# A three-instruction split of a row maximum, and the place of a tanh, in an attention kernel with a gated bilinear branch

## The chip, the cores and the metric

The kernel runs on one core of a Trainium2 chip. The metric is the device time of one execution in microseconds (us), the median of several runs. A core has five engines that run at the same time, each with its own instruction queue in order: TensorE (PE in the profile, with PEld for its weight loads), VectorE (DVE), ScalarE (ACT), GpSimd (POOL) and SyncE (SP), which here issues the DMAs.

## The reference

```python
xn = layernorm(x)                                # x: 2048 tokens x 512, fp32
qkv = xn @ wqkv                                  # 32 heads of 16
p = softmax(q @ k.T * 16 ** -0.5)                # for each head, 2048 x 2048
s = (p @ v) @ wo
h = (xn @ w_gate) * (xn @ w_up)                  # 2048 x 1792
g = silu(h @ w_down)
return x + s * g
```

All inputs and the output are fp32. `silu(y)` is computed as `y * (0.5 * tanh(y / 2) + 0.5)`.

## The kernel before, in words

**Splitting.** fp32 operands of matmuls are cut into a rounded high part (type fp32r) and a rest, and a product is made of high by high, high by low and low by high. For scores the three products stand under each other in 48 rows of one matmul (`KB = 48`). Two more rows of the contraction (`KR = 50`) take the row maximum off: the key side holds ones there, the query side the negated maximum, again as a rounded part and a rest.

**Units.** Heads are taken in 8 groups of four, queries in 4 chunks of 512: 32 units `i`. Each unit has 64 *positions*: 16 key tiles (`kt`) of 128 by four heads (`j`). `position` (function below) issues for each one a matmul `t` (keys by queries with the maximum, 50 rows, line L631) and its exponential on ScalarE into a tile `e` (L633), and, 86 positions ahead of it (`LEAD`), a matmul `s` for the scores of a later unit (48 rows, L609), whose maximum over 512 keys VectorE takes straight from PSUM into `MX` (L611). The matmuls `t` write to three rotating PSUM banks (`st`), the matmuls `s` to three others.

**Maxima.** When the last score of a unit has been reduced, `maxima(i)` reduces the four partial maxima of each row to the rounded and to the exact negated maximum (L617, L615), subtracts the two (L618, VectorE, both inputs in SBUF), turns the result by 32x32 blocks (L620), writes it to DRAM (`MD`) and reads it back as rows 48 and 49 of the query tile `qs`. The unit's first `t` stands 22 positions further on.

**Cycles.** The main loop runs 256 cycles. One cycle issues 7, 8 or 9 positions and spreads a share of *filler* matmuls between them (the projections of later heads, then the gated branch, then the output projection); the first and the last position of a cycle have no filler behind them. Then `values` runs what is due on other engines and `block`, the 16 matmuls `pv` (L644) of two key tiles with V. Their result goes to one of the three `st` banks as well and ScalarE copies it out: into the tile `part` (L655), which GpSimd adds to the sum `acc`, or, once for each unit, straight into `acc` (L650). A `pv` block needs the exponentials of its eight positions only, and the cycle's last position always lies behind these.

**The gated branch.** It runs over four chunks of tokens. The last step of a chunk adds two pairs of y tiles (L427), and then puts a generator `silu` on the list `later`: for each of the four token tiles a tanh on ScalarE (L362, from `y` into the tile `e2`, one buffer), two instructions on GpSimd (scale and shift, product with y) and, but for the last chunk, a store to DRAM (`YD`). `step_small(later)` takes one step of it; `position` calls it at `j == 3` and `kt % 4 == 2`, that is every 16 positions, ahead of that position's exponential, wherever in a cycle the position lies. The 16 tanhs lie between 634.39 and 1646.99 us of the span.

**Order.** PE, ACT, DVE and POOL run in the order in which the program is written. The queue of SP is ordered by the framework's scheduler. All SP and POOL instructions are issued from one helper line (L63).

**Constants.** `ones` (128x32) is set by GpSimd at the start; two rows of 2048 ones each are sent from it by DMA into rows 48 and 49 of the key tiles.

Of the kernel before, what the change touches and what calls it, by code (L numbers as in the profile page):

```python
# [11 lines left out]
F32 = mybir.dt.float32  # L12
# [36 lines left out]
def body(ctx, tc, x, wqkv, wo, wg, wu, wd, out):  # L49
# [45 lines left out]
    ones = keep.tile([P, 32], F32, name="ones")  # L95
    eps = keep.tile([P, 1], F32, name="eps")
    pool.memset(eps, 1e-5)
    pool.memset(ones, 1.0)
    V = keep.tile([P, NT, VCOLS], F32, name="V")

    def ones_columns(tts):
# [39 lines left out]
    def run_all(queue):  # L141
        while queue:
            queue.pop(0)()
# [467 lines left out]
        nc.vector.tensor_reduce(MX[i][:, j, t, kc:kc + 1], o, axis=AX.X, op=OP.max)  # L611

    def maxima(i):
        m = keep.tile([P, 4, 4], F32, name="m", bufs=2)
        nc.vector.tensor_reduce(m, MX[i], axis=AX.X, op=OP.max, negate=True)  # L615
        mm = keep.tile([P, 4, 2, 4], F32R, name="mm", bufs=2)
        nc.vector.tensor_reduce(mm[:, :, 0], MX[i], axis=AX.X, op=OP.max, negate=True)  # L617
        nc.vector.tensor_tensor(mm[:, :, 1], m, mm[:, :, 0], op=OP.subtract)  # L618
        mt = keep.tile([P, 32], F32, name="mt", bufs=2)
        nc.vector.transpose(mt, mm.rearrange("p j s t -> p (j s t)").bitcast(F32))  # L620
        dma(MD[i].rearrange("f (b q) -> b f q", b=4), mt)
        md = MD[i].rearrange("(p e s t) q -> e s p (t q)", p=2, e=2, s=2)
        for e in range(2):
            row = 64 * e + KB
            dma(QS[i][row:row + 2].bitcast(F32), md[e])
# [79 lines left out]

    def early():

        nc.scalar.activation(look, ones[0:1, 0:1], AF.Sqrt)
        for tt in range(4):
            load_x(tt)  # L710
        wraw = []
        for which in (1, 0):
            wraw.append(wtile(f"w{which}r"))
            dma(wraw[-1], wqkv[:, which * D:which * D + P].rearrange("(d p) f -> p d f", p=P))
        norm["raws"] = raws = [etile() if d < 3 else part_tile() for d in range(ND)]
        for d in range(ND):
            dma(raws[d], wqkv[d * P:(d + 1) * P, 2 * D:])
        for tt in range(4, NT):
            load_x(tt)

        def ahead(m):
            fst["qk", m] = qk_weights(m, 1), qk_weights(m, 0)

        def exp_table(_):
            nc.scalar.activation(look, ones[0:1, 0:1], AF.Exp)

        def warm(n):
            for _ in range(n):
                nc.tensor.matmul(psum("x", "warm"), ident, idle, start=True, stop=True)

        warm(4)
        first = (0, 1), (2, 3)
        for tts in first:
            ln_open(tts)
        ln_stats(0)
        ln_stats(1)
        ln_root(first[0])
        ln_scale(first[0])
        ln_apply(0)
        ln_apply(1)  # L740
        ln_stats(2)
        ln_stats(3)
        ln_turn(0)
        ln_turn(1)
        warm(3)
        ln_root(first[1])
        ln_scale(first[1])
        ln_apply(2)
        last = ln_apply(3)
        ln_low(0)  # L750
        ln_low(1)
        ln_turn(3)
        ln_turn(2)
        ln_low(3)
        ln_low(2)
        wk, wq = [split_raw(f"w{which}", raw, last) for which, raw in zip((1, 0), wraw)]
        wv = [[etile().bitcast(F32R) for _ in range(ND)] for _ in range(2)]
        for d in range(ND):
            nc.scalar.activation(wv[0][d], raws[d], AF.Copy)
            pool.tensor_tensor(wv[1][d], raws[d], wv[0][d], op=OP.subtract)  # L760

        def k(c):
            yield from qk_proj(wk, 0, 1, c, "f")
            load_k(0, [c])

        def q(c):
            yield from qk_proj(wq, 0, 0, c, "f" if c else "x")
            load_q(c)

        def v(*tts):  # L770
            for tt in tts:
                yield from v_proj(wv, tt, "f")

        at = {n: [] for n in range(253)}
        for c, stats, apply, turns in ((1, (0, 2, 4, 6), (26, 26, 26, 26), (38, 42, 46, 50)),
                                       (2, (16, 20, 26, 27), (60, 60, 62, 62), (70, 74, 79, 83)),
                                       (3, (30, 34, 36, 38), (73, 73, 85, 85), (100, 106, 112, 118))):
            for t in range(4):
                for n, fn in ((stats[t], ln_stats), (apply[t], ln_apply), (turns[t], ln_turn)):
                    at[n].append((fn, 4 * c + t))  # L780
        for tts, n, root, scale in ((tuple(range(4, 8)), 0, 13, 25), (tuple(range(8, NT)), 16, 52, 53)):
            at[n].insert(0, (ln_open, tts))
            at[root].append((ln_root, tts))
            at[scale].insert(0, (ln_scale, tts))
        at[190].append((ones_rows, ks[0]))
        at[150].append((exp_table, None))
        at[205].append((ahead, 1))
        at[130] += [(ones_columns, slice(8, NT)), (other_keys, None)]
        fst["v"] = v_proj(wv, NT - 1, "st")
        gens = [k(0), q(0), v(0, 1, 2), k(1), q(1), v(3), k(2), v(4, 5), k(3), v(*range(6, NT - 1))]  # L790
        scored = 0
        stream = (n for g in gens for n in g)
        for n in range(253):
            for fn, arg in at[n]:
                fn(arg)
            if n in EARLY:
                for _ in range(4 if n != EARLY[-1] else LEAD - scored):
                    score(scored, 0)
                    scored += 1
                if scored == 64:  # L800
                    maxima(0)
            next(stream, None)
        assert scored == LEAD
        return wq
# [29 lines left out]
    def step_small(q):  # L834
        if q and next(q[0], 1):
            q.pop(0)
# [70 lines left out]
            heads.append(finish(rounds[0][0]))  # L907
            step_small(heads)

    ready, reduced = {}, []  # L910

    def position(q):

        n, j = divmod(q, 4)
        i, kt = divmod(n, NT)
        g, c = divmod(i, NC)
        now[0] = n
        Tied.on = n < 18
        if j == 0:
            if kt == 8 and i + 2 < NU:  # L920
                load_q(i + 2)
            if kt == 0 and g + 1 < NG and c == 1:
                load_k(g + 1)
            ready[n] = i, kt, []
        if j == 3 and kt % 4 == 2:
            step_small(later)
        ready[n][2].append(expo(i, kt, j))
        scored = q + LEAD
        if scored < TOTAL:
            score(scored, 1)  # L930
        step()
        if j == 1:
            prepare()
        if scored < TOTAL and scored % (4 * NT) == 4 * NT - 1:
            reduced.append(lambda: maxima(scored // (4 * NT)))
# [3 lines left out]
    with tc.manual_schedule(engines=ORDERED):  # L939
        with banks_of(EARLY_BUFS):  # L940
            fil = Filler(filler(early()), spread)
        ctx.enter_context(banks_of(BUFS))
        run(fst["v"])
        q = 0
        while q < 4:
            position(q)
            q += 1
        for b in range(NU * NT // 2):
            if fil.done:
                parts = iter([3, 2, 3, 2, 2, 2, 1, 2])  # L950
                fil = Filler(ending(), lambda n: next(parts))
            work = fil.begin()
            if b >= NU * NT // 2 - 2:
                last = TOTAL - 4 * (NU * NT // 2 - 1 - b)
            else:
                fits = min(9, max(7, int(2.6 + 0.62 * work))) if q + LEAD < TOTAL and work else 8
                need = 8 * (b + 1)
                last = min(max(q + fits, need + AHEAD[0]), need + AHEAD[-1], TOTAL - 4)
            count = last - q
            fil.spread(max(2, count - 2))  # L960
            for k in range(count):
                position(q)
                q += 1
                if 0 < k < count - 1 or count < 3:
                    fil.part()
            if b < NU * NT // 2 - 1:
                values([ready.pop(2 * b), ready.pop(2 * b + 1)])
        run_all(before_values)
        while heads:
            step_small(heads)  # L970
        block([ready.pop(NU * NT - 2), ready.pop(NU * NT - 1)])
        run_all(behind_values)
        flush()
        while fil.left or not fil.done:
            now[0] += 1
            prepare()
            if not fil.left:
                fil.fetch()
            for _ in range(fil.left):
                next(fil.gen)  # L980
            fil.left = 0
            fil.fetch()
            flush()
# [17 lines left out]
```

## Time and profile before

| what | value |
|---|---|
| median of 3 runs | 1718.5 us (1717.84 to 1718.88) |
| the profiled execution's own time | 1718.17 us |
| its span | 1716.4 us (1.8 us lie around it) |
| granted clock of TensorE | 0.999 of full speed |
| busy: PE, DVE, ACT, POOL | 99%, 84%, 76%, 52% of the span |

A row of the page or of a group view names the line, the engine, the operation, what it writes and reads, the shape and the count; behind the bar stand the busy time in us, the mean of one in ns, and the idle time of the engine just before these instructions with what ended it. A row of the timeline begins with start and duration in us; idle time ahead of the instruction and its releaser stand in brackets. Since PE's matmuls are pipelined and their ends are modelled, PE reads as busy nearly everywhere, and time that it loses has to be read from the distance between its blocks: the copy of a `pv` block (L655 or L650) starts as the block ends, once a cycle, so the distance of two such copies is the length of a cycle.

### The profile page before, as it was taken

The page shows a single profiled execution, that of the slowest core. Times are in us where ns is not written, and L with a number is a line of the kernel's source. Part 1 is how long each engine was busy: PE and PEld are TensorE (multiplying, and loading weights), DVE is VectorE, ACT ScalarE, POOL GpSimd, SP SyncE. Part 2 cuts the span into 40 slices and gives each one's busy share as a digit, 9 for nine tenths or more (in the row PEclk, how much of TensorE's full clock was granted, in tenths as well). Part 3 has the DMA queues.
Part 4 walks back from the last instruction along what each step waited for, and adds up shares of the span by engine and source line. Part 5 has one row for each costly group of instructions (what it writes and reads, how often), then busy time and mean ns, then how long its engine had stood idle before and what let it go on. Part 6 is the DMA issues. An engine that isn't in the chain of part 4 may idle for free. (4 is left out here: it accounts for less than half of the span.)

```text
span 1716.4 us, 35005 instructions
## 1 busy us (share of the span) xinstructions
PE 1705.0 (99%) x13574; PEld 1042.5 (61%) x13574; DVE 1435.9 (84%) x2478; ACT 1307.4 (76%) x2568; POOL 885.4 (52%) x889
## 2 busy tenths in 40 slices
PE   8999999999999999999999999999999999999998
PEld 6666656666666665666656565666665666666655
DVE  6778888888888888888888888888888888898933
ACT  6358877877777778778777777887778787777774
POOL 5315445762644638446354572663637546446572
PEclk9999999999999999999999999999999999999999
DMA  6316633620241312412115220320225112011352
GB/s 210 106 48 201 243 115 125 152 66 19 64 91 36 107 47 73 89 47 60 30 52 133 64 74 23 92 71 27 64 75 125 54 36 73 27 54 48 121 177 79
DMA packets 117378, 145.79 MB, mean 85 GB/s; under 512 B 12636, under 2 KB 74332, under 8 KB 114524
## 3 DMA queue, kind: packets, MB, share of 16 engines
q1 hardware_dynamic: 117212, 143.55, 28.5%
q8 instruction: 107, 1.75, 0.4%
q14 instruction: 59, 0.48, 0.1%
HBM read 95.94 MB, written 47.45 MB: 84 GB/s over the span
## 5 line engine op out<-in xcount | busy, mean ns | idle before, releaser
L611 DVE TENSOR_REDUCE mx<-s 128x1 f32<-128x512 f32 x2048 | 1256.1, 683 | 212.3 <-PE s L609 177.4
L633 ACT ACTIVATE e<-t 128x512 f32<-128x512 f32 x2048 | 1100.1, 601 | 99.2 <-PE pv L644 47.4
L631 PE MATMUL t<-qs,ks 50*128 50x512 f32 x2048 | 783.4, 408 | 0.1
L609 PE MATMUL s<-ks,qs 48*128 48x512 f32 x2048 | 771.0, 410 | 0.6 <-DVE mx L611 0.5
L63 POOL TENSOR_TENSOR acc<-acc,part 128x512 f32<-128x512 f32 x214 | 276.3, 1291 | 610.2 <-ACT part L655 609.8
L631 PEld LDWEIGHTS t<-qs,ks 50*128 50x128 f32 x2048 | 359.1, 185 | 276.0 <-issue 118.6
L644 PE MATMUL pv<-e,V 128*32 128x512 f32 x4096 | 492.5, 598 | 0.0
L609 PEld LDWEIGHTS s<-ks,qs 48*128 48x128 f32 x2048 | 350.6, 185 | 28.8 <-issue 5.4
L655 ACT ACTIVATE part<-pv 128x512 f32<-128x512 f32 x214 | 128.1, 599 | 209.7 <-PE pv L644 209.7
L644 PEld LDWEIGHTS pv<-e,V 128*32 128x32 f32 x4096 | 107.0, 109 | 242.0 <-issue 215.9
L289 PE MATMUL g<-fh,w1h 64*128 64x512 f32 x224 | 90.5, 404 | 0.0
L285 PE MATMUL u<-fh,w0h 64*128 64x512 f32 x224 | 90.4, 404 | 0.0
L289 PE MATMUL y<-dh,hh 64*128 64x512 f32 x224 | 89.6, 400 | 0.0
L285 PE MATMUL y<-dh,hh 64*128 64x512 f32 x224 | 88.9, 397 | 0.0
L289 PE MATMUL u<-fh,w0l 64*128 64x512 f32 x224 | 88.2, 394 | 0.0
L289 PE MATMUL g<-fl,w1h 64*128 64x512 f32 x224 | 88.0, 393 | 0.0
L285 PE MATMUL g<-fl,w1h 64*128 64x512 f32 x224 | 88.0, 393 | 0.0
L285 PE MATMUL u<-fh,w0l 64*128 64x512 f32 x224 | 88.0, 393 | 0.0
L285 PE MATMUL u<-fl,w0h 64*128 64x512 f32 x224 | 88.0, 393 | 0.0
L289 PE MATMUL g<-fh,w1l 64*128 64x512 f32 x224 | 87.9, 393 | 0.0
L285 PE MATMUL g<-fh,w1h 64*128 64x512 f32 x224 | 87.9, 392 | 0.0
L289 PE MATMUL u<-fl,w0h 64*128 64x512 f32 x224 | 87.8, 392 | 0.0
(262 smaller groups left out, 2987.5 us busy)
## 6 DMA issues: line engine op xcount, KB each, us to landing
w1r<-in_wg_dram SPq DMA_DIRECT2D x56, 256.0 KB
w0r<-in_wu_dram SPq DMA_DIRECT2D x56, 256.0 KB
wdr<-in_wd_dram SPq DMA_DIRECT2D x56, 256.0 KB
qs<-QD SPq DMA_DIRECT2D x64, 192.0 KB
ks<-KD SPq DMA_DIRECT2D x12, 768.0 KB
KD<-hl SPq DMA_DIRECT2D x16, 512.0 KB
QD<-hl SPq DMA_DIRECT2D x16, 512.0 KB
OD<-acc SPq DMA_DIRECT2D x31, 256.0 KB
```

The source lines that it names most:

```text
L63: got = getattr(self.engine, name)(*args, **kw)
L285: nc.tensor.matmul(outs[k], l[LOWER], r[LOWER], start=k == 0 and n == 0, stop=(stop or k == 0) and n == len(low) - 1, skip_group_check=k == 1)
L289: nc.tensor.matmul(outs[1 - k], l[UPPER], r[UPPER], start=k == 0 and m == 0, stop=(stop or k == 0) and m == len(high) - 1, skip_group_chec ...
L609: nc.tensor.matmul(o, QS[i][b:b + KB, pr, t * P:(t + 1) * P], k[b:b + KB, pr, kc * 512:(kc + 1) * 512], start=True, stop=True)
L611: nc.vector.tensor_reduce(MX[i][:, j, t, kc:kc + 1], o, axis=AX.X, op=OP.max)
L631: nc.tensor.matmul(o, k[b:b + KR, pr, kt * P:(kt + 1) * P], QS[i][b:b + KR, pr], start=True, stop=True)
L633: nc.scalar.activation(e, o, AF.Exp, scale=DH ** -0.5)
L644: nc.tensor.matmul(o[32 * j:32 * j + 32], V[:, kt, h0:h0 + 32], es[j], start=n == 0, stop=n == len(todo) - 1)
L655: nc.scalar.activation(part, o, AF.Copy)
```

## The change

**The maxima.** The third instruction is no longer a subtraction of two tiles. The rounded maximum is now kept positive (`mm[:, 1]`), the exact one negated (`mm[:, 2]`), both in one tile, and the rest is a reduction (sum) over pairs of these two (`mm[:, 0]`, a view in which the two members of a pair lie 16 elements apart). So the query tile's row 48 holds the rest and row 49 the positive rounded maximum, which meets a row of minus ones on the key side: the lower half of `ones` is set to -1. The order of the rows in DRAM changes with it; the DMAs keep their sizes. The tiny table-loading activations read `eps` instead of `ones`.

**The tanh.** `position` no longer takes the step of `silu` itself but puts it on a list `gates`, which the main loop empties ahead of a cycle's last position, so ahead of its last exponential.

```diff
-    pool.memset(ones, 1.0)
+    pool.memset(ones[0:64], 1.0)
+    pool.memset(ones[64:P], -1.0)
...
     def maxima(i):
-        m = keep.tile([P, 4, 4], F32, name="m", bufs=2)
-        nc.vector.tensor_reduce(m, MX[i], axis=AX.X, op=OP.max, negate=True)
-        mm = keep.tile([P, 4, 2, 4], F32R, name="mm", bufs=2)
-        nc.vector.tensor_reduce(mm[:, :, 0], MX[i], axis=AX.X, op=OP.max, negate=True)
-        nc.vector.tensor_tensor(mm[:, :, 1], m, mm[:, :, 0], op=OP.subtract)
+        mm = keep.tile([P, 3, 4, 4], F32R, name="mm", bufs=2)
+        nc.vector.tensor_reduce(mm[:, 1], MX[i], axis=AX.X, op=OP.max)
+        nc.vector.tensor_reduce(mm[:, 2].bitcast(F32), MX[i], axis=AX.X, op=OP.max, negate=True)
+        with nc.allow_low_precision(reason="the rest of a rounded maximum"):
+            nc.vector.tensor_reduce(mm[:, 0], mm[:, 1:3].rearrange("p s j t -> p j t s").bitcast(F32), axis=AX.X, op=OP.add)
         mt = keep.tile([P, 32], F32, name="mt", bufs=2)
-        nc.vector.transpose(mt, mm.rearrange("p j s t -> p (j s t)").bitcast(F32))
+        nc.vector.transpose(mt, mm[:, 0:2].rearrange("p s j t -> p (s j t)").bitcast(F32))
         dma(MD[i].rearrange("f (b q) -> b f q", b=4), mt)
-        md = MD[i].rearrange("(p e s t) q -> e s p (t q)", p=2, e=2, s=2)
+        md = MD[i].rearrange("(s p e t) q -> e s p (t q)", p=2, e=2, s=2)
...
-    ready, reduced = {}, []
+    ready, reduced, gates = {}, [], []
...
         if j == 3 and kt % 4 == 2:
-            step_small(later)
+            gates.append(lambda: step_small(later))
...
             for k in range(count):
+                if k == count - 1:
+                    run_all(gates)
                 position(q)
...
         run_all(before_values)
+        run_all(gates)
```

ScalarE around the first tanh of the first chunk, before (`e<-t` is an exponential, named by key tile and head; `part<-pv` the copy of a block; `look` a one-element read that keeps ScalarE in step):

```order
L633 ACTIVATE e<-t_10_0_9403 128x512
L633 ACTIVATE e<-t_10_1_9418 128x512
L633 ACTIVATE e<-t_10_2_9427 128x512
L655 ACTIVATE part_9455<-pv_9446 128x512
L362 ACTIVATE e_9458<-y 128x512
L633 ACTIVATE e<-t_10_3_9463 128x512
L633 ACTIVATE e<-t_11_0_9470 128x512
L633 ACTIVATE e<-t_11_1_9481 128x512
L293 ACTIVATE look<-u_0_9378 1x1
```

The same stretch of ScalarE's order in the changed kernel (its lines are one higher):

```order
L634 ACTIVATE e<-t_8_1_9293 128x512
L634 ACTIVATE e<-t_8_2_9304 128x512
L363 ACTIVATE e_9332<-y 128x512
L634 ACTIVATE e<-t_8_3_9337 128x512
L656 ACTIVATE part<-pv_9346 128x512
L634 ACTIVATE e<-t_9_0_9358 128x512
L634 ACTIVATE e<-t_9_1_9365 128x512
L634 ACTIVATE e<-t_9_2_9378 128x512
L634 ACTIVATE e<-t_9_3_9389 128x512
```

The tanh stood ahead of the first exponential of a cycle; it now stands ahead of the last one of the cycle before that. (A step asked for before the chunk's end is now taken after it, at the end of that cycle, so that all 16 tanhs come 8 or 9 positions sooner.)

VectorE at one of the 32 maxima, before:

```order
L611 TENSOR_REDUCE mx<-s_1_3_11069 128x1
L615 TENSOR_REDUCE m<-mx 128x16
L617 TENSOR_REDUCE mm<-mx 128x4x4
L618 TENSOR_TENSOR mm<-m,mm 128x4x4
L620 STREAM_TRANSPOSE mt<-mm 128x32
L611 TENSOR_REDUCE mx<-s_1_2_11098 128x1
```

And in the changed kernel:

```order
L612 TENSOR_REDUCE mx<-s_1_3_11057 128x1
L616 TENSOR_REDUCE mm<-mx 128x16
L617 TENSOR_REDUCE mm<-mx 128x16
L619 TENSOR_REDUCE mm<-mm 128x16
L621 STREAM_TRANSPOSE mt<-mm 128x32
L612 TENSOR_REDUCE mx<-s_1_2_11085 128x1
```

The place and the count are the same; the instruction with two inputs has become one with one input of 32 elements. The order of PE is the same in both kernels.

On SP, where the weights of the gated branch (`w1r`, `w0r`, `wdr`), the gates' stores (`YD`), the maxima (`MD`, `qs<-MD`) and the sums (`OD`) share one queue, the end of the first chunk read before:

```order
L63 DMA w1r<-in_wg_dram 128x4x128
L63 DMA w0r<-in_wu_dram 128x4x128
L63 DMA OD_120<-acc 128x512
L63 DMA MD_98<-mt 4x32x32
L63 DMA YD_123<-y 128x512
L63 DMA qs<-MD_98 2x2x512 x2
L63 DMA wdr<-in_wd_dram 128x512
```

And now:

```order
L63 DMA YD_123<-y 128x512
L63 DMA w1r<-in_wg_dram 128x4x128
L63 DMA w0r<-in_wu_dram 128x4x128
L63 DMA OD_120<-acc 128x512
L63 DMA MD_98<-mt 4x32x32
L63 DMA wdr<-in_wd_dram 128x512
L63 DMA qs<-MD_98 2x2x512 x2
```

The store moved ahead of the two weight loads, and a load took its place between the maxima's two transfers.

More of the change, by code (lines that the diff above doesn't have):

```diff
@@ L706, in early @@
     def early():
-        nc.scalar.activation(look, ones[0:1, 0:1], AF.Sqrt)
+        nc.scalar.activation(look, eps[0:1], AF.Sqrt)
         for tt in range(4):
@@ L724, in exp_table @@
         def exp_table(_):
-            nc.scalar.activation(look, ones[0:1, 0:1], AF.Exp)
+            nc.scalar.activation(look, eps[0:1], AF.Exp)
         def warm(n):
```

## The prediction

> **What bounds the kernel now.** I read the page first: which engine has no time to spare, and what the others wait for.
>
> ```profile
> span 1716.4 us, 35005 instructions
> ## 1 busy us (share of the span) xinstructions
> PE 1705.0 (99%) x13574; PEld 1042.5 (61%) x13574; DVE 1435.9 (84%) x2478; ACT 1307.4 (76%) x2568; POOL 885.4 (52%) x889
> ...
> L611 DVE TENSOR_REDUCE mx<-s 128x1 f32<-128x512 f32 x2048 | 1256.1, 683 | 212.3 <-PE s L609 177.4
> ...
> L655 ACT ACTIVATE part<-pv 128x512 f32<-128x512 f32 x214 | 128.1, 599 | 209.7 <-PE pv L644 209.7
> ```
>
> TensorE is busy for 99%, and VectorE (212.3 us idle ahead of the score reductions) and ScalarE (209.7 us ahead of the copies of `pv`) mostly wait for it. So the kernel is as long as TensorE's queue, plus what that queue stands still for one of the others. As the order of PE does not change, the change can only pay, or cost, through such standstills. The page hides them. The second view is therefore ScalarE's timeline over the end of the first chunk, for the length of each cycle from copy to copy.
>
> ```profile
> 627.35 0.60 ACT L633 ACTIVATE e<-t 128x512 f32<-128x512 f32 x1 [0.85 <-PE pv L644]
> 628.32 0.60 ACT L655 ACTIVATE part<-pv 128x512 f32<-128x512 f32 x1 [0.37 <-PE pv L644]
> ...
> 633.90 0.60 ACT L655 ACTIVATE part<-pv 128x512 f32<-128x512 f32 x1 [1.35 <-PE pv L644]
> 634.39 0.62 ACT L362 ACTIVATE e<-y 128x512 f32<-128x512 f32 x1
> 634.91 1.57 ACT L633 ACTIVATE e<-t 128x512 f32<-128x512 f32 x3
> ...
> 639.98 0.60 ACT L655 ACTIVATE part<-pv 128x512 f32<-128x512 f32 x1 [1.27 <-PE pv L644]
> ...
> 646.01 0.60 ACT L655 ACTIVATE part<-pv 128x512 f32<-128x512 f32 x1 [0.86 <-PE pv L644]
> ...
> 653.01 0.60 ACT L655 ACTIVATE part<-pv 128x512 f32<-128x512 f32 x1 [1.30 <-PE pv L644]
> ...
> 658.53 0.63 ACT L362 ACTIVATE e<-y 128x512 f32<-128x512 f32 x1
> ...
> 659.92 0.60 ACT L650 ACTIVATE acc<-pv 128x512 f32<-128x512 f32 x1 [0.27 <-PE pv L644]
> ...
> 665.49 0.60 ACT L655 ACTIVATE part<-pv 128x512 f32<-128x512 f32 x1 [1.29 <-PE pv L644]
> ...
> 671.05 0.60 ACT L655 ACTIVATE part<-pv 128x512 f32<-128x512 f32 x1 [1.28 <-PE pv L644]
> ...
> 672.02 0.63 ACT L362 ACTIVATE e<-y 128x512 f32<-128x512 f32 x1
> ...
> 677.33 0.60 ACT L655 ACTIVATE part<-pv 128x512 f32<-128x512 f32 x1 [0.76 <-PE pv L644]
> ...
> 684.31 0.60 ACT L655 ACTIVATE part<-pv 128x512 f32<-128x512 f32 x1 [1.30 <-PE pv L644]
> ...
> 691.50 0.60 ACT L655 ACTIVATE part<-pv 128x512 f32<-128x512 f32 x1 [0.37 <-PE pv L644]
> ```
>
> Undisturbed cycles give the yardsticks: with seven positions 671.05 - 665.49 = 5.56 us, with eight 646.01 - 639.98 = 6.03, with nine 684.31 - 677.33 = 6.98. Three cycles between these rows are longer than their kind: 6.08 with seven positions (to 639.98; a tanh at its head), 6.28 with eight (to 677.33; a tanh near its head), 7.19 with nine (to 691.50; no tanh). The first two belong to one half of the change, the third to the other.
>
> **The tanh: what is taken away.** The first tanh of a chunk stands between the copy and the first of seven exponentials. It holds them back by 634.91 - 634.39 = 0.52 us, and in a cycle this short in filler ScalarE does not catch up: 6.08 - 5.56 = 0.52 us are lost. All four chunks have this tanh at this place. The last one, and the other tanh near the head of an eight-position cycle (in the second chunk), read:
>
> ```profile
> 997.11 0.60 ACT L655 ACTIVATE part<-pv 128x512 f32<-128x512 f32 x1 [1.29 <-PE pv L644]
> ...
> 1003.38 0.60 ACT L655 ACTIVATE part<-pv 128x512 f32<-128x512 f32 x1 [0.76 <-PE pv L644]
> ...
> 1611.56 0.60 ACT L650 ACTIVATE acc<-pv 128x512 f32<-128x512 f32 x1 [1.29 <-PE pv L644]
> ...
> 1617.63 0.60 ACT L655 ACTIVATE part<-pv 128x512 f32<-128x512 f32 x1 [1.27 <-PE pv L644]
> ```
>
> The last: 1617.63 - 1611.56 = 6.07, so 0.51 lost; four of them at 0.51 make 2.0 us. The two in eight-position cycles: 6.28 - 6.03 = 0.25 and 6.27 - 6.03 = 0.24, together 0.5 us. The second tanh of a chunk stands in a nine-position cycle with much filler: 653.01 - 646.01 = 7.00 against 6.98, nothing. The third stands ahead of a last exponential already (658.53), and its cycle, 659.92 - 653.01 = 6.91, is no longer than its kind. In all the tanhs now cost 2.5 us.
>
> **The tanh: what it costs at the new place.** What hides it there is the `pv` block, for whose end ScalarE waits before the copy. The last exponential is not read by that block, so the block is not held up; the copy is, only if tanh and exponential fill more than that idle time. ScalarE needs 0.52 us for the tanh. Idle there were 0.85 us ahead of the last exponential for the first tanh (627.35), and 1.27, 1.30 and 1.29 us ahead of the copy for the other three (639.98, 653.01, 665.49). It fits everywhere. I take nothing; the bounds are 0 and 0.52 us for each of 16. Next late at the head of the freed cycle is the matmul `t` itself, as in any cycle of its kind. The tanh's input is no new wait: the first reads a tile whose sum stands more than a cycle earlier on VectorE, the others wait for the gate before them to leave GpSimd, about two cycles earlier.
>
> GpSimd's two instructions and the store move along; a row of GpSimd's timeline and one of the groups:
>
> ```profile
> 629.06 1.29 POOL L63 TENSOR_TENSOR acc<-acc,part 128x512 f32<-128x512 f32 x1 [5.66 <-ACT part L655]
> ```
>
> ```profile
> L63 POOL TENSOR_TENSOR y<-e,y 128x512 f32<-128x512 f32 x16 | 20.6, 1288 | 1.3
> ```
>
> The first gate now runs in the 5.66 us in which GpSimd was idle ahead of the sum at 629.06, and takes 1.29 us for the product and half as much for the scaling. Later gates run in front of a sum or of weight casts instead of behind them, with the same total. On SP the first store, which waits for GpSimd, now heads two weight loads; these wait for GpSimd's casts of the weights before them, which stand behind that gate in its queue anyway. I price both moves at nothing, with 0 to 0.5 us as bounds.
>
> **The maxima.** VectorE's third instruction of 128x16 elements should take as long each time. It does not (count, minimum, median and maximum in ns):
>
> ```profile
> L617 DVE TENSOR_REDUCE mm<-mx x32: 201/207/211, 83.9 to 1637.0; 128x16 fp32r<-128x64 f32 x32
> L618 DVE TENSOR_TENSOR mm<-m,mm x32: 174/176/1078, 84.2 to 1637.2; 128x16 fp32r<-128x16 f32 x32
> ```
>
> The timelines of GpSimd and VectorE show why:
>
> ```profile
> 683.77 1.29 POOL L63 TENSOR_TENSOR w0l<-w0r,w0h 128x512 fp32r<-128x512 f32 x1
> ...
> 683.85 0.20 DVE L617 TENSOR_REDUCE mm<-mx 128x16 fp32r<-128x64 f32 x1
> 684.09 0.99 DVE L618 TENSOR_TENSOR mm<-m,mm 128x16 fp32r<-128x16 f32 x1
> ...
> 1535.97 1.07 DVE L618 TENSOR_TENSOR mm<-m,mm 128x16 fp32r<-128x16 f32 x1
> ```
>
> The subtraction at 684.09 ends at 685.08, just as GpSimd's product of two SBUF tiles, begun at 683.77, is over (685.06): it was held until GpSimd had finished. The reduction of one SBUF tile at 683.85 ran inside the same GpSimd instruction in its ordinary 0.20 us, and none of 32 took over 0.211. So one input runs beside GpSimd and two do not. The Trainium skill states this ("SBUF — State Buffer", section "Who interferes with whom"): two SBUF inputs contend with GpSimd's reads, and a reduction never does on trn2; the trace agrees, with 1078 ns against 211 ns at most.
>
> Six of the 32 subtractions are held to over 0.7 us, the first at 684.09, the last at 1535.97; the cycle behind the first is the long one above. The second and the fourth of the six:
>
> ```profile
> 784.63 0.60 ACT L655 ACTIVATE part<-pv 128x512 f32<-128x512 f32 x1 [1.30 <-PE pv L644]
> ...
> 791.90 0.60 ACT L655 ACTIVATE part<-pv 128x512 f32<-128x512 f32 x1 [0.37 <-PE pv L644]
> ...
> 1335.93 0.60 ACT L655 ACTIVATE part<-pv 128x512 f32<-128x512 f32 x1 [1.27 <-PE pv L644]
> ...
> 1342.40 0.60 ACT L655 ACTIVATE part<-pv 128x512 f32<-128x512 f32 x1 [0.86 <-PE pv L644]
> ```
>
> The score reductions behind the held instruction start late, their PSUM banks come free late, and TensorE stands: 7.19 - 6.98 = 0.21 us at 684, 7.27 - 6.98 = 0.29 at 784, 6.47 - 6.03 = 0.44 at 1336 (eight positions). The other three are like that at 784 (nine positions, held by over 1 us): 0.87. Sum: 1.8 us. Shorter holds, under 0.6 us, I put at nothing; two of them lie in the long cycles counted above.
>
> The new reduction reads 32 elements 16 apart; no row shows such a one. Bounds: below, the unheld subtraction's 0.174 us; above, the 0.211 us of the reduction of 64 elements. I take 0.2, the row of its own kind: 32 times about 0.03 us more on VectorE, 1 us in all, beside the 212.3 us that it sits idle for TensorE, so nothing on the path. The Trainium skill speaks against such a swap: "VectorE: DVE Perf Modes", section "Rules for kernel authors", calls the reduction the slowest VectorE operation and advises restructuring it away. By that rule, taken as fully on the path, the gain would be 1 us less; the rows (207 against 176 ns) bear out the slowness, not the place on the path.
>
> **The start.** One memset becomes two, on GpSimd ahead of the tile that TensorE's warming matmuls wait for.
>
> ```profile
> 0.91 0.12 POOL L63 MEMSET ones<- 128x32 f32 x1
> ...
> 2.40 5.29 PE L729 MATMUL warm<-acc,ident 128*128 128x512 f32 x8 [2.40 <-POOL acc L63]
> ```
>
> Each memset also waits for the one before. I take 0.1 us, bounds 0 and 0.3.
>
> **Sum.** 2.5 + 1.8 - 0.1 = 4.2 us off the profiled execution's 1718.17, so 1714.0. The median of the runs lies 0.3 us above that execution, so the forecast for the median is 1718.5 - 4.2 = 1714.3 us.
>
> **The rivals.** A: *the tanh's stall only moves.* The freed cycles lose their time elsewhere, for instance to the later last exponential, whose bank is due at the second `t` of the next cycle. Then the 1.8 us of the maxima remain, less 0.1: 1716.8. For it: the last exponential does come 0.52 us later. Against it: the third tanh, which already stands so and costs nothing.
>
> B: *the reductions stay late.* The strided pair reduction is slow or is held as well, or VectorE's lag has other reasons. Then only the tanh's 2.5 us come, less 0.1: 1716.1. For it: the operation is in no row. Against it: 0.211 us at most for its kind in 32 cases.
>
> C: *slower, by the new place itself.* The tanh in front of the last exponential pushes the copy of `pv` and with it the bank that the next cycle's third `t` needs. This decides as soon as the idle time at the copy is under 0.52 us in the changed kernel, for example because ScalarE arrives later at the cycle's end than in this trace. Price: 16 x 0.52 = 8.3 us, against 4.3 gained: 1722.6 with the start. The copy at 628.32 has only 0.37 idle ahead of it, so the mechanism is near in one place of each chunk; but 0.85 us lie ahead of its exponential.
>
> D: *no effect.* The standstills are taken up by later waits and the end stays where it is: 1718.5. Against it, TensorE's 99%.
>
> **How the numbers follow.** My forecast gets 0.70, A 0.10, B 0.09, C 0.05, D 0.06. The forecast's own range follows from its bounds: a start at no cost and a few tenths for the short holds give 1713.2; 0.3 for the start, 0.5 for the queues and a tanh that costs in the four tight places (0.1 to 0.2 each) give 1715.6. A change of 0.2%, 3.4 us, is about what a measurement of this kernel can tell from no change, so faster means below 1715.1. Of the forecast's 0.70 about 0.62 lies below that; B and A with smaller losses than priced add 0.07: 0.69. Slower by over 0.2% is C, with 0.01 for something unseen: 0.06. The rest, 0.25, is the same. The range runs from 1713.2 to 1716.8, which takes in A and B and leaves out C, D and the tails.
>
> **What would show it.** Right: the third instruction at all 32 maxima within 0.17 to 0.25 us, also under a running GpSimd product; the cycles that held 0.99 and 1.07 us subtractions back at 6.98; the seven-position cycles at the chunks' ends at 5.56, with the tanh in the idle time ahead of the copy; the idle time before those copies about 0.5 us smaller. Wrong: new cycles longer than their kind at the tanhs' new places (A or C), the reduction over 0.3 us (B), or cycles restored and the span unchanged (D).

## The result and the profile after

| | before | changed |
|---|---|---|
| median of 12 runs, us | 1718.97 (1717.84 to 1719.30) | 1714.64 (1713.69 to 1715.28) |
| ratio, with its 95% interval | | 0.9976 (0.9969 to 0.9984) |
| profiled execution, us | 1718.17 | 1715.28 |
| its span, us | 1716.4 | 1713.4 |

The change takes 4.3 us off the median; 4.2 were forecast, and the median stands 0.3 us above the forecast time. The page of the changed kernel, its head and two groups:

```profile
span 1713.4 us, 35012 instructions
## 1 busy us (share of the span) xinstructions
PE 1701.9 (99%) x13574; PEld 1043.7 (61%) x13574; DVE 1430.9 (84%) x2478; ACT 1309.0 (76%) x2568; POOL 884.9 (52%) x890
...
L656 ACT ACTIVATE part<-pv 128x512 f32<-128x512 f32 x214 | 128.1, 599 | 205.1 <-PE pv L645 205.1
```

TensorE is still the bound, with the same 13574 matmuls. ScalarE's idle time ahead of the copies fell from 209.7 to 205.1 us: the tanhs fill some of it now. ScalarE's timeline over the end of the first chunk shows where:

```profile
628.77 0.60 ACT L634 ACTIVATE e<-t 128x512 f32<-128x512 f32 x1 [0.35 <-PE pv L645]
629.74 0.60 ACT L656 ACTIVATE part<-pv 128x512 f32<-128x512 f32 x1 [0.37 <-PE pv L645]
...
635.30 0.60 ACT L656 ACTIVATE part<-pv 128x512 f32<-128x512 f32 x1 [1.33 <-PE pv L645]
...
638.99 0.62 ACT L363 ACTIVATE e<-y 128x512 f32<-128x512 f32 x1
639.51 0.59 ACT L634 ACTIVATE e<-t 128x512 f32<-128x512 f32 x1
640.86 0.60 ACT L656 ACTIVATE part<-pv 128x512 f32<-128x512 f32 x1 [0.76 <-PE pv L645]
...
671.89 0.60 ACT L656 ACTIVATE part<-pv 128x512 f32<-128x512 f32 x1 [1.28 <-PE pv L645]
...
677.93 0.60 ACT L656 ACTIVATE part<-pv 128x512 f32<-128x512 f32 x1 [0.87 <-PE pv L645]
...
684.90 0.60 ACT L656 ACTIVATE part<-pv 128x512 f32<-128x512 f32 x1 [1.31 <-PE pv L645]
...
691.86 0.60 ACT L656 ACTIVATE part<-pv 128x512 f32<-128x512 f32 x1 [0.37 <-PE pv L645]
```

The three cycles that were too long are back at their kind: 640.86 - 635.30 = 5.56 us (6.08 before), 677.93 - 671.89 = 6.04 (6.28 before), 691.86 - 684.90 = 6.96 (7.19 before). The tanh at 638.99 stands ahead of a last exponential, and the idle time ahead of the copy behind it is 0.76 us, where it was 1.27: the 0.51 us that the tanh takes. At the chunk's first tanh the idle time shrank ahead of the exponential, from 0.85 to 0.35, and the copy's 0.37 stayed. (Counted in exponentials, the 16 tanhs come 8 to 10 sooner, not 8 or 9.)

The tile view of the maxima (count, minimum, median and maximum in ns), and then VectorE and GpSimd in the timeline at the place of the first held subtraction:

```profile
L617 DVE TENSOR_REDUCE mm<-mx x32: 200/208/215, 85.4 to 1633.9; 128x16 f32<-128x64 f32 x32
L619 DVE TENSOR_REDUCE mm<-mm x32: 186/188/190, 85.7 to 1634.2; 128x16 fp32r<-128x32 f32 x32
```

```profile
684.43 1.28 POOL L63 TENSOR_TENSOR w0l<-w0r,w0h 128x512 fp32r<-128x512 f32 x1
684.44 0.21 DVE L617 TENSOR_REDUCE mm<-mx 128x16 f32<-128x64 f32 x1
684.68 0.19 DVE L619 TENSOR_REDUCE mm<-mm 128x16 fp32r<-128x32 f32 x1
```

The pair reduction took 186 to 190 ns at all 32 maxima. At 684.68 it ran from end to end inside GpSimd's instruction on two SBUF tiles, where VectorE's subtraction had been held for 0.99 us. (GpSimd makes the low part `w0l` of a weight there, by a subtraction; the prediction calls it a product.)

Where the time went, by cycles, here from the first matmul of one block to that of the next: the cycles with the four first tanhs took 6.08, 6.00, 6.07 and 6.00 us before and take 5.55, 5.50, 5.60 and 5.50 now (from copy to copy all four took 6.06 to 6.08 before); the two in eight-position cycles went from 6.28 to 6.04; together 2.5 us. The six cycles behind held subtractions went from 7.20, 7.28, 7.28, 6.47, 7.26 and 7.26 to 6.96 (6.04 for the fourth): 1.9 us.

That TensorE stood for ScalarE in the first kind and for VectorE in the second can be read from its weight loads. In the kernel before, the first long cycle has this row in the timeline, idle time and releaser in brackets; at that place of the changed kernel's cycle no load waits for an exponential:

```profile
635.55 0.18 PEld L631 LDWEIGHTS t<-qs,ks 50*128 50x128 f32 x1 [0.38 <-ACT e L633]
```

And this is the row of the waits view (us in all, times, longest in us) for loads of the scores' matmuls that waited for a score reduction, before and then changed. There are six waits fewer:

```profile
PEld s L609 <- DVE mx L611: 4.5, 13, 1.0
```

```profile
PEld s L610 <- DVE mx L612: 3.2, 7, 1.0
```

The rows of the `pv` block, before and then changed, give the sum, since they stand from the first block to the last:

```profile
L644 PE MATMUL pv<-e,V x4096: 592/592/619, 108.2 to 1703.6; 128*32 128x512 f32 x196
```

```profile
L645 PE MATMUL pv<-e,V x4096: 592/592/619, 109.7 to 1700.6; 128*32 128x512 f32 x196
```

1595.4 us became 1590.9: 4.5 less. The profiled pair differs by only 2.9, because the first block of the changed execution came 1.5 us later. That head is taken up below.

### The profile page after: what moved, and what is told of

Its sections match the earlier page's. It is cut to its first block, busy times and chain, and to the rows that moved or that the text cites. A ratio compares the mean times of both kernels' runs of the same rounds, so it can differ in the third digit from the quotient of the medians.

```text
span 1713.4 us, 35012 instructions
## 1 busy us (share of the span) xinstructions
PE 1701.9 (99%) x13574; PEld 1043.7 (61%) x13574; DVE 1430.9 (84%) x2478; ACT 1309.0 (76%) x2568; POOL 884.9 (52%) x890
## 5 line engine op out<-in xcount | busy, mean ns | idle before, releaser
L656 ACT ACTIVATE part<-pv 128x512 f32<-128x512 f32 x214 | 128.1, 599 | 205.1 <-PE pv L645 205.1
L290 PE MATMUL g<-fh,w1l 64*128 64x512 f32 x224 | 88.0, 393 | 0.0
L290 PE MATMUL u<-fl,w0h 64*128 64x512 f32 x224 | 87.8, 392 | 0.0
L286 PE MATMUL g<-fh,w1l 64*128 64x512 f32 x224 | 87.8, 392 | 0.0
```

Source lines behind the costliest of these rows:

```text
L286: nc.tensor.matmul(outs[k], l[LOWER], r[LOWER], start=k == 0 and n == 0, stop=(stop or k == 0) and n == len(low) - 1, skip_group_check=k == 1)
L290: nc.tensor.matmul(outs[1 - k], l[UPPER], r[UPPER], start=k == 0 and m == 0, stop=(stop or k == 0) and m == len(high) - 1, skip_group_chec ...
L656: nc.scalar.activation(part, o, AF.Copy)
```

## The experiments

The theory has two independent parts (the tanh's place, and a VectorE instruction with two SBUF inputs under GpSimd's reads). The rivals were those of the prediction: a stall that only moves, a lag of other origin, a price at the new place. Behind each time stand its lowest and highest run, then the ratio with its 95% interval. Times stand beside the kernel before on the same chip: 1718.87 us in the first four experiments, 1718.75 in the next four, 1718.73 in the last three.

### The tanh's place alone

The kernel before with the second half of the change only:

```diff
-            step_small(later)
+            gates.append(lambda: step_small(later))
...
+                if k == count - 1:
+                    run_all(gates)
                 position(q)
```

> The kernel before with the tanh's new place alone; the maxima keep their subtraction of two tiles. Theory (each half gives back its own standstills of TensorE, and they add up): the cycles behind the chunks' ends fall from about 6.05 to 5.55 us and two of eight positions from 6.28 to 6.04, in all 2.5 us less than before, ratio 0.9985; the six long holds of the subtraction stay, within 0.75 to 1.08 us, with their cycles at 7.2 to 7.3. Rival (the tanh's stall only moves): no gain, ratio 1.000, new long cycles at the tanhs' new places.

1716.07 us (1715.15 to 1716.68), 0.9984 (0.9976 to 0.9993): 2.8 us less. The tanh cycles are all restored (5.55, 5.50, 5.55, 5.50; 6.04, 6.05). Five of the six others stay long. In ScalarE's timeline the first of them is 691.27 - 684.00 = 7.27 us:

```profile
684.00 0.60 ACT L655 ACTIVATE part<-pv 128x512 f32<-128x512 f32 x1 [1.31 <-PE pv L644]
...
691.27 0.60 ACT L655 ACTIVATE part<-pv 128x512 f32<-128x512 f32 x1 [0.37 <-PE pv L644]
```

The sixth, the eight-position one, fell from 6.47 to 6.11. With the gate's GpSimd instructions moved away, GpSimd's instruction on `wdr` and `dh` there starts earlier against the subtraction, which is held for only 0.39 us (GpSimd's and VectorE's rows of the timeline):

```profile
1333.51 1.29 POOL L63 TENSOR_TENSOR dl<-wdr,dh 128x512 fp32r<-128x512 f32 x1
...
1334.44 0.39 DVE L618 TENSOR_TENSOR mm<-m,mm 128x16 fp32r<-128x16 f32 x1
```

So 2.5 us of tanh and 0.36 of one hold make the 2.8.

### The maxima alone

The changed kernel with the gates issued where they were:

```diff
-            gates.append(lambda: step_small(later))
+            step_small(later)
```

> The kernel before with the new maxima and the row of minus ones alone; the tanh stays where it was. Theory: the six cycles behind held subtractions fall to their kind's length, in all 1.9 us less than before, ratio 0.9989; the long cycles at the tanhs stay at about 6.0 and 6.28. Rival (VectorE's lag has another reason than the two inputs): ratio 1.000, the cycles stay at 7.2 to 7.3.

1716.90 us (1716.34 to 1717.62), 0.999 (0.9981 to 0.9998): 2.0 us less. All six cycles are back at 6.96 (or 6.05), and the tanh's cycles are as long as before, 640.02 - 633.95 = 6.07 us in ScalarE's timeline:

```profile
633.95 0.60 ACT L656 ACTIVATE part<-pv 128x512 f32<-128x512 f32 x1 [1.35 <-PE pv L645]
...
640.02 0.60 ACT L656 ACTIVATE part<-pv 128x512 f32<-128x512 f32 x1 [1.27 <-PE pv L645]
```

Each half brings its own cycles back and leaves the other's alone. That the halves sum to 4.8 and the whole gives 4.3 is explained as far as the 0.36 us of the eight-position cycle, which both halves free; the rest is within the intervals.

### An extra instruction of two inputs, and one of one input

The changed kernel with a 128x16 sum beside the pair reduction, whose result is not used, once with two SBUF inputs:

```diff
+        junk = keep.tile([P, 4, 4], F32, name="junk", bufs=2)
+        nc.vector.tensor_tensor(junk, mm[:, 1].bitcast(F32), mm[:, 2].bitcast(F32), op=OP.add)
         mt = keep.tile([P, 32], F32, name="mt", bufs=2)
```

> The changed kernel with one more VectorE instruction at each of the 32 maxima: a sum of two SBUF tiles of 128x16, whose result nobody reads. Theory (held by GpSimd because of the second SBUF input): the extra instruction takes 0.17 us where GpSimd reads nothing and up to 0.9 us where it does; the same five or six cycles go back to 7.1 to 7.3 (6.3 to 6.5 with eight positions), in all 1.2 to 1.9 us more than the changed kernel. Rival (any further instruction costs its own time at most): 0.17 to 0.2 us at all 32, no cycle longer by 0.1, the time that of the changed kernel.

And once with the same numbers read as one input:

```diff
+        nc.vector.tensor_reduce(junk, mm[:, 1:3].rearrange("p s j t -> p j t s").bitcast(F32), axis=AX.X, op=OP.add)
```

> The control for the run before: the changed kernel with one more VectorE instruction at each of the 32 maxima that reads one SBUF tile, the reduction over pairs a second time, result not read. Theory: 0.19 us at all 32 places, no cycle longer by more than 0.1 us, the time that of the changed kernel within 0.3 us. Rival (the plain length of VectorE's chain at the maxima sets TensorE's standstill): the cycles behind a maximum grow by 0.1 to 0.2 us each, 3 to 6 us in all.

Two inputs: 1715.12 us (1714.43 to 1715.79), 0.9979 (0.9969 to 0.9988). One input: 1713.75 (1713.56 to 1714.47), 0.9972 (0.9962 to 0.9983). Neither total came as expected: with two inputs the time is 0.5 us above the changed kernel's 1714.64, not 1.2 to 1.9, and with one it is 0.9 below it, not within 0.3. The instruction itself and the cycles behind it say more. The tile views, two inputs first:

```profile
L621 DVE TENSOR_TENSOR junk<-mm x32: 159/166/999, 85.6 to 1634.3; 128x16 f32<-128x16 f32 x32
```

```profile
L621 DVE TENSOR_REDUCE junk<-mm x32: 173/177/181, 84.8 to 1632.7; 128x16 f32<-128x32 f32 x32
```

With one input none of 32 took over 181 ns, and no cycle grew by more than 0.07 us. With two, the median is lower (166 ns), but five were held for 970 to 999 ns, and the five cycles behind them grew by 0.18 to 0.23, 1.05 us together. The timeline of the two-input kernel at the first:

```profile
683.99 1.29 POOL L63 TENSOR_TENSOR w0l<-w0r,w0h 128x512 fp32r<-128x512 f32 x1
...
684.33 0.98 DVE L621 TENSOR_TENSOR junk<-mm 128x16 f32<-128x16 f32 x1
684.44 0.60 ACT L658 ACTIVATE part<-pv 128x512 f32<-128x512 f32 x1 [1.30 <-PE pv L647]
...
691.60 0.60 ACT L658 ACTIVATE part<-pv 128x512 f32<-128x512 f32 x1 [0.37 <-PE pv L647]
```

The instruction begun at 684.33 ends at 685.31, and GpSimd's at 685.28. The cycle is 691.60 - 684.44 = 7.16 us, against 6.96. Place and data are the same in both kernels, but the operation differs too: a sum of two tiles here, a reduction there. A row of the kernel before tells these apart in one case. VectorE's products of a PSUM tile and an SBUF tile (L356) have two inputs as well; one of them, at 320.24, began inside a GpSimd instruction on two SBUF tiles (319.65, for 1.29 us) and ended before it in its ordinary 0.68 us, and none of the 56 took over 0.683. So two inputs alone were not held there; every held instruction here read two SBUF tiles. The Trainium skill ("SBUF — State Buffer", section "Who interferes with whom") has GpSimd and VectorE's second read port share one lock; both traces agree, with 999 ns against 181 ns at most.

The five cycles are not the whole difference. By the rows of the `pv` block, the stretch from the first block to the last takes 1591.1 us with two inputs and 1590.3 with one, against 1590.9 in the changed kernel (1590.6 when run again). So against the one-input kernel the two inputs cost 0.8 us, and against the changed kernel hardly any: the other cycles are shorter by a few hundredths each in both extra-instruction kernels, and why is open. The rest of the 1.4 us between the medians goes with the head of the span (below), where the profiled one-input execution began its transposes 0.8 us earlier, at 7.98 us against 8.77.

### How much room the new place has

The changed kernel with the tanh issued twice, and then three times, into the same tile:

```diff
-            nc.scalar.activation(e, y[:, t], AF.Tanh, scale=0.5)
+            for _ in range(2):
+                nc.scalar.activation(e, y[:, t], AF.Tanh, scale=0.5)
```

> The changed kernel with each of the 16 tanhs issued twice into the same tile, at the new place. Theory (the time hides in the idle time at the end of the cycle): two tanhs need 1.04 us; there are 1.22 us (0.85 and 0.37) at the first and 1.27 to 1.35 at the others, so no cycle grows by over 0.1 us and the time is that of the changed kernel within 0.5 us; the idle time ahead of the copies falls from about 0.76 to 0.25 us. Rival (any ScalarE time at this place is paid by TensorE): 16 times 0.52, 8 us more.

> The changed kernel with each tanh issued three times at the new place. Theory: 1.56 us no longer fit into 1.22 to 1.35, so the copies and with them the banks come 0.2 to 0.35 us late, and cycles grow by up to that at most of the 16 places: 1 to 5 us more than the changed kernel, and no idle time is left ahead of those copies. Rival (the place costs nothing whatever stands there, because the copy is never urgent): no cycle longer than its kind, the time that of the changed kernel.

Two: 1714.16 us (1713.52 to 1715.37), 0.9974 (0.9964 to 0.9985), no cost. Three: 1722.90 (1722.1 to 1723.4), 1.0023 (1.0014 to 1.0032), 8.3 us above the changed kernel. ScalarE's timelines, two and then three:

```profile
638.65 1.28 ACT L364 ACTIVATE e<-y 128x512 f32<-128x512 f32 x2
639.84 0.58 ACT L635 ACTIVATE e<-t 128x512 f32<-128x512 f32 x1
640.51 0.60 ACT L657 ACTIVATE part<-pv 128x512 f32<-128x512 f32 x1
```

```profile
635.82 0.60 ACT L657 ACTIVATE part<-pv 128x512 f32<-128x512 f32 x1 [1.34 <-PE pv L646]
...
639.51 1.95 ACT L364 ACTIVATE e<-y 128x512 f32<-128x512 f32 x3
641.36 0.58 ACT L635 ACTIVATE e<-t 128x512 f32<-128x512 f32 x1
641.84 0.59 ACT L657 ACTIVATE part<-pv 128x512 f32<-128x512 f32 x1
...
648.00 0.60 ACT L657 ACTIVATE part<-pv 128x512 f32<-128x512 f32 x1 [0.86 <-PE pv L646]
```

With two, the copy starts 0.67 us behind the exponential's start, when ScalarE's own spacing is 0.48 (641.84 - 641.36): some 0.2 us of room are left here, and the cycle is as long as in the changed kernel. With three, none is left, and the time is lost: from the copy at 635.82 to the second copy behind it are 12.18 us, and 646.91 - 635.30 = 11.61 in the changed kernel. That is rival C: its mechanism exists, and it decides where the idle time at the cycle's end runs out, 1.27 us here. One tanh of 0.52 us is far from it.

The size was missed. At most 0.35 us a gate was expected, from three times 0.52; 0.31 to 0.60 were measured. Three tanhs into one tile take 641.36 - 639.51 = 1.85 us, and 1.85 - 1.27 = 0.58 is about what two cycles lost here (0.57).

### The tanh at the cycle's head

```diff
-                if k == count - 1:
+                if k == 0:
                     run_all(gates)
```

> The changed kernel with the list of gates emptied ahead of a cycle's first position instead of its last: the same 16 tanhs, each later by one exponential and one block. Theory (the place decides, and there the filler of the cycle): six of them come to the head of seven-position cycles, 0.4 to 0.5 us each, three to eight positions with little filler, 0.24 each, the rest to cycles with much filler, nothing; about 3.5 us more than the changed kernel. Rival (what paid was that the gates run earlier and out of GpSimd's way): the time of the changed kernel, no cycle longer than its kind.

1719.00 us (1718.06 to 1719.77), 1.0001 (0.9992 to 1.001): the whole gain is gone, 4.4 us more than the changed kernel, of which the cycles show 4.1; about 3.5 were expected. How it is spread was not as expected. Seven-position cycles, thought to lose 0.4 to 0.5 us, lost 0.17 to 0.24; eight-position ones, thought to lose 0.24, lost 0.15 to 0.71, most of them over 0.4; and nine-position ones, thought to be free, lost 0.21 to 0.24. ScalarE's timeline:

```profile
640.98 0.60 ACT L656 ACTIVATE part<-pv 128x512 f32<-128x512 f32 x1 [1.27 <-PE pv L645]
641.47 0.62 ACT L363 ACTIVATE e<-y 128x512 f32<-128x512 f32 x1
...
647.47 0.60 ACT L656 ACTIVATE part<-pv 128x512 f32<-128x512 f32 x1 [0.84 <-PE pv L645]
```

The eight-position cycle with the tanh right behind its copy takes 647.47 - 640.98 = 6.49 us, 0.45 over its kind, while ScalarE still has 0.84 us idle at its end. So the place within the cycle costs, not the tanh's 0.52 us of work: at 642.63 a weight load of a matmul `t` waits 0.62 us for an exponential. Why the loss goes by other lengths than thought was not settled: in the kernel before the tanh stood with a fixed position, not always with the cycle's first.

### The head of the span

The changed kernel with the memset for which the warming matmuls wait moved ahead of the others:

```diff
     eps = keep.tile([P, 1], F32, name="eps")
+    idle = keep.tile([P, 512], F32, name="acc", bufs=2)
+    pool.memset(idle, 0.0)
     pool.memset(eps, 1e-5)
...
-    idle = keep.tile([P, 512], F32, name="acc", bufs=2)
-    pool.memset(idle, 0.0)
```

> The changed kernel with the memset of the tile that TensorE's warming matmuls read issued as the first of GpSimd's memsets behind the identity's, instead of the last. Theory (the head of the span varies by up to 1.5 us with the moment at which the granted clock goes up, which follows the first matmul): the first warming matmul starts at about 1.5 to 1.8 us instead of 2.7, the full clock comes earlier, the first transposes start at 7.5, bounded by ScalarE's layer norm, and the median falls by 0.5 to 1 us with a smaller spread. Rival (the clock goes up at moments of its own): the transposes still start anywhere from 7.5 to 9.1, the median that of the changed kernel within 0.3 us.

1713.67 us (1713.23 to 1714.30), 0.997 (0.9959 to 0.9981). To tell a gain from the changed kernel's own spread, both were run side by side, with a kernel that delays the same matmuls by issuing that memset three times:

```diff
     pool.memset(idle, 0.0)
+    pool.memset(idle, 0.0)
+    pool.memset(idle, 0.0)
```

> The changed kernel once more, unaltered, beside the next two on the same chip. Theory: 1714.6 us within 0.3, single runs spread over 1.5 us, because the first transposes start anywhere from 7.5 to 9.1 us.

> The kernel with the early memset once more. Theory (an earlier first matmul brings the full clock earlier): 0.7 to 1.1 us under the changed kernel on the same chip, spread of single runs under 1.1 us. Rival (the difference of the last call was chance): within 0.3 us of the changed kernel.

> The dose in the other direction: the changed kernel with that memset issued three times, so that TensorE's first matmul waits about 1 us longer (start at 3.7 us). Theory: the full clock and the first transposes come up to 1 us later, the median rises by 0.6 to 1.1 us, to 1715.2 to 1715.7. Rival (the clock goes up at its own moments): the median of the changed kernel within 0.3 us.

The changed kernel again: 1714.25 us (1713.87 to 1715.57), 0.9974 (0.9964 to 0.9984), just below the 1714.3 to 1714.9 expected. Memset first: 1713.85 (1713.61 to 1714.51), 0.9971 (0.996 to 0.9982). Memset late: 1715.65 (1714.94 to 1716.58), 0.9981 (0.9972 to 0.999). The late kernel lies within the 1715.2 to 1715.7 expected; its distance from the changed kernel, 1.4 us, is more than the 0.6 to 1.1 expected. The early one is 0.4 below it, between the 0.7 to 1.1 expected and the rival's 0.3 at most. Pooled, the changed kernel has a median of 1714.46 us (20 runs) and the memset first 1713.76 (14 runs). The spread is smaller too, but the runs overlap, and the kernel with one extra input, whose head is that of the changed kernel, reached 1713.75 (7 runs). A gain from the early memset is likely rather than shown.

TensorE's timelines at the head: the changed kernel, the memset first (its second run), the memset late.

```profile
2.70 6.52 PE L730 MATMUL warm<-acc,ident 128*128 128x512 f32 x8 [2.70 <-POOL acc L63]
9.05 1.04 PE L246 MATMUL xT<-ident,ks 128*128 128x128 f32 x8
```

```profile
1.78 5.80 PE L730 MATMUL warm<-acc,ident 128*128 128x512 f32 x8 [1.78 <-POOL eps L63]
7.42 1.04 PE L246 MATMUL xT<-ident,ks 128*128 128x128 f32 x8
```

```profile
3.87 6.68 PE L732 MATMUL warm<-acc,ident 128*128 128x512 f32 x8 [3.87 <-POOL acc L63]
10.38 1.04 PE L248 MATMUL xT<-ident,ks 128*128 128x128 f32 x8
```

The first transposes `xT` stand behind the eight warming matmuls, and start at 9.05, 7.42 and 10.38 us.

## Why the prediction was right

- **TensorE's standstills as the only lever.** Right: the cycles fell by 4.5 us, and these are the cycles that were named.
- **The tanh, 2.5 us.** Measured 2.5, in the six cycles named, and with that half alone 2.8 with 0.36 of it from a hold that it shortened. This effect on a subtraction was not in the prediction; in the whole change it has no effect, since nothing is held there.
- **Nothing at the new place.** Right: the idle time shrank by 0.51 us and no cycle grew. Two tanhs fit as well, and a third costs 8.3 us. Rival C fell for its size, not its mechanism. The bound of 0.1 to 0.2 us in the four tight places was not needed, since the last exponential's wait gave way and the copy's did not change.
- **Moved GpSimd work and stores, nothing.** No cycle is longer than before by more than 0.06 us; it was not tested by itself.
- **The maxima, 1.8 us.** Measured 1.9. The pair reduction took 188 ns (taken: 0.2 us, bounds 0.174 to 0.211) and was never held, so B fell. By the rule of the Trainium skill that was weighed against this ("VectorE: DVE Perf Modes", section "Rules for kernel authors") the gain should have been 1 us less; the reductions are slower than a free subtraction, as it says (188 against 176 ns), but 32 more of them cost no time that the run with one extra input shows.
- **A and D.** Both halves alone keep their gain, and the span followed the cycles: neither happened.
- **The start, 0.1 us: a size that was off.** The first warming matmul came at 2.70 us instead of 2.40, the bound's 0.3. It was also the wrong thing to ask: what the first transposes wait for is the end of the warming matmuls, and this moves by more than that from one execution to the next. The median fell by 4.3 us where the cycles fell by 4.5, which leaves 0.2 for the head; no run isolates the start's share. That the total came within 0.1 us of the forecast is in part luck, since the head of a single execution moves by more than that.

## What to carry to other kernels

Where one engine is busy for 99%, compare cycles of equal content: the ones that are longer than their kind name the standstills that are left, and each can be priced by subtraction. A step of a waiting engine belongs where that engine is going to wait anyway, ahead of its last piece of a cycle; how many such steps fit is the idle time there, to be read before moving more. A small VectorE instruction whose longest run is many times its median is held by something: look at what GpSimd is doing when it ends, and try a form that reads one SBUF tile.

## What the runs showed of the hardware

TensorE becomes fast at a moment that differs from one execution to the next. In the weight loads this is a step from 0.34 us to 0.19 (the warming matmuls) and 0.14 (the transposes). The weight-load rows of the timeline, before and then changed:

```profile
5.12 0.34 PEld L729 LDWEIGHTS warm<-acc,ident 128*128 128x128 f32 x1 [0.52 <-issue]
5.81 0.19 PEld L729 LDWEIGHTS warm<-acc,ident 128*128 128x128 f32 x1 [0.35 <-issue]
```

```profile
7.98 0.34 PEld L730 LDWEIGHTS warm<-acc,ident 128*128 128x128 f32 x1 [0.52 <-issue]
8.62 0.14 PEld L246 LDWEIGHTS xT<-ident,ks 128*128 128x128 f32 x1 [0.31 <-issue]
```

The first such load stands 3.4 us behind TensorE's first one in the kernel before, and 5.9 in the changed one. By the same reading, in us:

| kernel | first load | first fast load | between | first `xT` |
|---|---|---|---|---|
| before | 2.40 | 5.81 | 3.4 | 7.53 |
| changed | 2.69 | 8.62 | 5.9 | 9.05 |
| changed, again | 2.70 | 7.94 | 5.2 | 8.80 |
| one extra input | 2.70 | 6.27 | 3.6 | 7.98 |
| maxima alone | 2.71 | 5.99 | 3.3 | 7.71 |
| memset first | 1.78 | 5.87 | 4.1 | 7.59 |
| memset first, again | 1.78 | 6.13 | 4.4 | 7.42 |
| memset late | 3.86 | 9.95 | 6.1 | 10.38 |

Between 3.3 and 6.1 us pass, whatever the kernel. The trace's record of the granted clock fits: it begins with full speed at 5.63 us before, at 8.41 in the changed kernel and at 9.88 with the memset late, and in all 13 traces between the last slow load's start and the first fast load's. What was granted ahead of it is not recorded; the views count that stretch as full speed. With the 0.3 us by which the first load came later, this accounts for the 1.5 us by which the head of the two profiled executions differs, and that is as large as the spread of the runs of one kernel (1717.84 to 1719.30). It is likely the cause of that spread; the runs without a profile don't show it. With an early first matmul the transposes can come to wait for ScalarE rather than for TensorE's pace. TensorE's timeline of the first run with the memset first shows it (in the second, at 7.42, they did not wait):

```profile
7.59 1.09 PE L246 MATMUL xT<-ident,ks 128*128 128x128 f32 x8 [0.28 <-ACT ks L235]
```

The Trainium skill ("TensorE: Matmul & The Clock Gate", Part 1: The HAM clock gate) tells of a window of 3.4 us that runs free of the kernel's start, and of a faster clock after one busy window. The traces agree with the window: their stretches at full speed last 1703.251, 1706.664 or 1710.077 us, 3.413 apart. They agree in kind with the wait, as 3.3 to 6.1 us is from about one window to less than two. They don't agree with the 500 ns by which the page lets that moment vary.

A second surprise: tanhs that ScalarE writes back to back into the same tile start 0.65 us apart (with three, the exponential follows 1.85 us behind the first), while a single tanh holds the exponential behind it back by 0.52, and the exponential and the copy behind it, into other tiles, are 0.48 us apart. No run tells whether the shared tile is the reason.
